# A fused linear-attention and channel-mix kernel: 1/rms from column-tiled sums of squares, spread by DMA, in a new order of work

## The chip, the core and the metric

The kernel runs on one core of one Trainium2 chip. The metric is device microseconds (us) from launch to end of one execution. Engines are called PE (TensorE), ACT (ScalarE), DVE (VectorE), POOL (GpSimd) and SP (SyncE). Each works through its own list of instructions in order. Semaphores tie the lists together.

## The reference, cut to what matters

Two stages are computed, for 8 batches (B), 8 heads (H), 576 tokens (S) and a head width of 64 (D):

```python
kv  = einsum('bhsd,bhse->bhde', k, v)
o   = einsum('bhsd,bhde->bhse', q, kv)
rms = sqrt(mean(o * o, axis=-1, keepdims=True) + 1e-06)     # per batch, head and token
x   = (o / rms * g_norm), heads side by side: (B, S, 512)
x_prev = x shifted by one token, zero at the start
xk  = mu_k * x + (1 - mu_k) * x_prev ;  xr = mu_r * x + (1 - mu_r) * x_prev
out = sigmoid(xr @ w_r) * (relu(xk @ w_k) ** 2 @ w_v)       # w_k: 512x1024, w_v: 1024x512
```

The change is about `rms`: for each token and head a sum over 64 squares, then 1/sqrt, then a product with all 64 elements of that head.

## The kernel before, in words

**Layout.** All data is held transposed: partitions are channels. The four pairs of heads (`NHP = 4`) each fill 128 partitions, 64 for either head, and are held two at a time: z = 0 holds pairs 0 and 1, z = 1 pairs 2 and 3.

**Order of work.** No scheduler runs. The kernel builds small named pieces, each a function with its dependencies, and `Plan.emit` issues them in exactly the order of the words in the string `ORDER`. A suffix @A or @D says that ACT or DVE does the piece. So each engine's list, the queue of loads on POOL and the queue of stores on SP are written out by hand in that one string. The words, for batch b, half z and token half i:

- `ld.q b.z`, `ld.k`, `ld.v`: loads from HBM, cast to bf16, issued by POOL (L247). Batches 0 and 1 load by halves z, the others whole. `ld.wk0/1`, `ld.wr`, `ld.wv0/1` load the weights (L262). `g.wk`, `g.wr` scale them by g_norm.
- `kv b`: 72 matmuls of 64x64 tiles (L282), `kc` copies the result out of PSUM. `q b.z`: 36 transposes of 64x64 (L290), `qc` copies.
- `u b.zi`: four 64x64 matmuls over 288 tokens, one section of o (L297). `uc` casts it to SBUF, `sq` squares it (L351 on ACT, L353 on DVE).
- `ss b.hp`: the sum of squares (L435). The weights are `ones`, 128x128, with 1/64 in two diagonal blocks, so every one of a head's 64 partitions gets that head's mean. Two matmuls of 288 tokens per pair of heads hp, four such words per batch from batch 1 on. Batch 0 does it by sections (L412).
- `rs b.hp`: 1/sqrt on ACT straight from PSUM (L302), 128x576 per pair of heads.
- `mul b.z`: x = o times 1/rms on DVE (L403). `wr` copies the wrap column block. `d` takes the difference to the previous token (L314), `mk`/`mr` scale it by mu (L178 on ACT, L180 on DVE), `xk`/`xr` add (L327), into a ring that holds four batches.
- `k g.fc`: x times w_k for a group g of 512 tokens (9 groups in all), four matmuls of 512 columns per word (L513; L489 for group 0). `relu` (L474), `ksq` the square (L523). `r g.ci` (L535) and `sig` (L545): the gate. `v g.ci.part` (L555): times w_v. `out` (L568, L582 in the last group): product with the gate. `st`: the stores (L464), issued by SP.
- `z:512`: a matmul of zeros, 512 columns (L453), into a PSUM tile that is not read.

**Memory that ties words together.** PSUM has two buffers "at" (u, q, kv, ss) and two buffers "mm" (k, r, v). SBUF has three buffers each for q, k, v, `sq` and `rs`, two for `sqk`. A word that needs a buffer waits for the last reader of what was in it. In the last group both column halves of `v8.3` share one PSUM tile.

**Pace.** A batch's q, k, v are loaded several batches ahead, as buffers come free. Group g can start when the batches under its 512 tokens have their `xk`. The table for 1/sqrt and the one for the sigmoid are loaded in turn on ACT (L188).

Of the kernel before, what the change touches and what calls it, by code (L numbers as in the profile page):

```python
# [20 lines left out]
g.wk11@D ss0.11 k0.010 d0.0b mr0.0a@A mul0.10 d0.1a mk0.1a@A g.wk00@D ld.wv0 rs0.11 z:512 z:512 k0.000 xk0.1a
g.wk01@D mk0.0b@A ld.wv1 mul0.11 k0.011 wr0.0@D xk0.0b d0.1b k0.001 relu0.01 ld.q2.01 mk0.1b@D q1.1 xk0.1b relu0.00
q1.0 mr0.1b@D k0.110 d0.0w xr0.0a mk0.0w@A mr0.1a@D wr0.1@A k0.111 xr0.1a ld.k2.01 g.wr1@D k0.100 mr0.0w@D relu0.11
ksq0.01 k0.101 g.wr0@D ld.v2.01 xr0.0w xr0.1b r0.0 mr0.0b@D relu0.10 xr0.0b ld.q3.01 r0.1 qc1.1@D qc1.0@A d0.1w r0.2
mr0.1w@D ld.v4.01 xk0.0w ksq0.00 r0.3 ksq0.11 sig0.0 mk0.1w@D ld.k3.01 kv1 xk0.1w ksq0.10 kc1@A u1.00 u1.11 sq1.00@A
# [5 lines left out]
ksq1.1 k1.6 relu1.2 xr1.1 ss2.3 k1.7 rs2.2 ksq1.2 rs2.3 r1.0 relu1.3 mul2.1 r1.1 wr2.1@D d2.1 q3.1 kv3 mr2.1@D q3.0
ld.k6.01 qc3.1@D r1.2 sig1.0 ld.q6.01 mk2.1@D ss2.1 qc3.0@A kc3@D r1.3 ksq1.3 v1.2.0 xk2.1 sig1.1 v1.3.0 v1.2.1
rs2.1 v1.3.1 mul2.0 u3.01 q4.1 out1.1 wr2.0@A v1.1.0 sq3.01@A uc3.01@A v1.1.1 qc4.1@D st1.2 d2.0 u3.11 u3.00
uc3.11@A v1.0.0 st0.3 mk2.0@D uc3.00@A sq3.11@D v1.0.1 sq3.00@A xk2.0 u3.10 ss3.0 sq3.10@A uc3.10@D k2.0 rs3.0
out1.0 ss3.1 k2.1 rs3.1 st1.1 ss3.3 mul3.0 k2.2 rs3.3 mr2.0@D st1.0 wr3.0@A ss3.2 relu2.0 k2.3 xr2.0 d3.0 rs3.2
st1.3 kv4 xr2.1 relu2.1 q4.0 ld.v7.01 q5.1 qc4.0@D k2.4 kc4@A ld.k7.01 qc5.1@A ksq2.1 k2.5 ld.q7.01 ksq2.0 ld.v6.01
mul3.1 u4.00 relu2.2 u4.11 k2.6 wr3.1@D uc4.00@D sq4.11@A k2.7 ksq2.2 r2.2 sq4.00@D relu2.3 uc4.11@D r2.3 d3.1
mr3.0@D u4.01 kv5 uc4.01@D q5.0 r2.0 sq4.01@D sig2.1 qc5.0@D u4.10 r2.1 kc5@A uc4.10@D ss4.1 sq4.10@D sig2.0 v2.1.0
ksq2.3 mk3.0@D ss4.3 v2.0.0 mr3.1@D mk3.1@D v2.0.1 rs4.1 xk3.0 v2.2.0 rs4.3 u5.11 u5.00 sq5.11@A uc5.11@D v2.1.1
uc5.00@A xr3.1 v2.2.1 out2.0 ss4.2 v2.3.0 rs4.2 sq5.00@D st2.0 v2.3.1 xk3.1 mul4.1 ss4.0 st2.1 k3.0 rs4.0 out2.1  # L40
q6.1 u5.10 qc6.1@D k3.1 st2.2 sq5.10@A uc5.10@A wr4.1@D k3.4 d4.1 relu3.0 st2.3 ss5.2 k3.5 rs5.2 ksq3.0 k3.2 xr3.0
relu3.2 mul4.0 k3.3 mk4.1@A mr4.1@D r3.0 ksq3.2 wr4.0@A relu3.1 r3.1 d4.0 mr4.0@D u5.01 kv6 xk4.1 q6.0 k3.6 qc6.0@D
sig3.0 k3.7 uc5.01@A kc6@A r3.2 sq5.01@D relu3.3 ksq3.1 r3.3 xr4.0 ss5.3 ksq3.3 sig3.1 ss5.1 v3.3.0 xr4.1 v3.3.1
mk4.0@D v3.2.0 rs5.3 v3.2.1 rs5.1 mul5.1 u6.11 out3.1 u6.00 uc6.11@A v3.1.0 uc6.00@A v3.1.1 sq6.11@D st3.3 wr5.1@A
xk4.0 ss5.0 v3.0.0 rs5.0 st3.2 sq6.00@A v3.0.1 u6.01 u6.10 uc6.01@A r4.0 uc6.10@A sq6.01@D r4.1 out3.0 sq6.10@A q7.1
kv7 st3.0 q7.0 r4.2 sig4.0 kc7@D mul5.0 r4.3 qc7.0@A d5.1 k4.2 mk5.1@D sig4.1 k4.3 wr5.0@A d5.0 k4.0 relu4.1 xk5.1
k4.1 qc7.1@A mk5.0@D k4.4 relu4.0 k4.5 mr5.0@A ksq4.0 k4.6 ksq4.1 k4.7 relu4.2 xk5.0 ss6.3 relu4.3 ksq4.2 ss6.2
v4.3.0 ksq4.3 v4.2.0 xr5.0 v4.2.1 rs6.3 v4.3.1 rs6.2 mul6.1 ss6.0 ss6.1 rs6.0 v4.0.0 mr5.1@D rs6.1 out4.1 v4.0.1
u7.11 u7.00 st4.2 uc7.11@D v4.1.0 uc7.00@A wr6.1@A sq7.00@D sq7.11@A v4.1.1 st4.3 u7.10 out4.0 u7.01 uc7.10@A k5.0
st3.1 uc7.01@A k5.1 sq7.10@D sq7.01@D d6.1 ss7.3 ss7.2 rs7.3 k5.2 mul6.0 relu5.0 k5.3 rs7.2 ksq5.0 ss7.1 k5.6  # L50
relu5.1 wr6.0@D mk6.1@D ss7.0 k5.7 mr6.1@A xk6.1 xr5.1 k5.4 relu5.3 mul7.1 k5.5 ksq5.1 r5.0 wr7.1@D relu5.2 d7.1
r5.1 mk7.1@D rs7.0 ksq5.3 v5.1.0 rs7.1 ksq5.2 v5.0.0 d6.0 v5.1.1 mul7.0 sig5.0 xr6.1 v5.0.1 wr7.0@A mr7.1@A r5.2
out5.0 r5.3 mk6.0@D st5.0 v5.3.0 mr6.0@D sig5.1 v5.2.0 xr6.0 st5.1 xk6.0 v5.3.1 st4.0 v5.2.1 r6.0 st4.1 out5.1 r6.1
xr7.1 st5.2 k6.4 sig6.0 d7.0 k6.5 k6.2 relu6.2 k6.3 ksq6.2 k6.0 xk7.1 relu6.1 mr7.0@D k6.1 xr7.0 r6.2 relu6.0
mk7.0@D r6.3 ksq6.1 xk7.0 k6.6 sig6.1 ksq6.0 k6.7 k8.2 relu6.3 k8.3 ksq6.3 v6.2.0 relu8.1 v6.3.0 ksq8.1 v6.3.1
v6.1.0 v6.0.0 v6.2.1 v6.1.1 out6.1 v6.0.1 k7.0 out6.0 k7.1 st6.1 r7.2 relu7.0 r7.3 st6.0 k7.2 sig7.1 st6.3 k7.3
st5.3 k8.4 relu7.1 k8.5 st6.2 ksq7.1 k7.4 ksq7.0 relu8.2 k7.5 k7.6 relu7.2 k7.7 ksq7.2 k8.0 relu7.3 k8.1 ksq7.3
v7.3.0 ksq8.2 v7.2.0 relu8.0 v7.2.1 ksq8.0 v7.3.1 v8.1.00 out7.1 k8.6 st7.3 k8.7 r7.0 st7.2 relu8.3 r7.1 ksq8.3
v7.0.0 sig7.0 v7.0.1 v7.1.0 v7.1.1 r8.0 out7.0 r8.1 st7.0 r8.2 sig8.0 r8.3 st7.1 v8.1.10 sig8.1 v8.2.00 out8.10
v8.2.10 st8.10 v8.0.00 out8.20 v8.0.10 st8.20 v8.3.00 out8.00 v8.3.10 v8.3.01 st8.00 out8.30 v8.3.11 st8.30 out8.31  # L60
st8.31
# [562 lines left out]
```

## Time and profile before

| | |
|---|---|
| time, median of 3 runs | 214.93 us (214.77 to 215.88) |
| the profiled execution's own time | 216.15 us |
| its span, first to last instruction | 214.4 us |
| around the span | 1.75 us |
| mean granted TensorE clock | 0.984 |
| PE busy | 198.5 us, 93% of the span |
| PE weight loads busy | 100.6 us, 47% |
| DVE busy | 135.0 us, 63% |
| ACT busy | 136.0 us, 63% |
| POOL busy | 26.2 us, 12% |
| moved by DMA | 26.55 MB |
| instruction fetches (queue q8) | 17, 0.28 MB |

How to read it: busy time is the union of an engine's instructions. The profile's second part cuts the span in 40 slices of 5.36 us and gives the busy tenths of each engine, the clock that PE was granted and the share of the DMA engines. The chain of work that ended last goes back from the end to what released each step; the word "issue" there is time in which the engine waited for no semaphore that the profile shows.

### The profile page before, as it was taken

To read this page: it belongs to the slowest core of one execution; us is meant where nothing else is said; L and a number is where in the kernel's file an instruction comes from. 1 tells how busy PE (TensorE), PEld (TensorE's weight loads), DVE (VectorE), ACT (ScalarE), POOL (GpSimd) and SP (SyncE) were. 2 spreads that over 40 slices of the span, in tenths; PEclk is the share of its full clock that TensorE was granted. 3 is DMA by queue.
4 is the path that set the end of the run, shared out by engine and by line. 5 is a ranking of instruction groups with operands and counts; after the bars stand their busy time and mean duration, and the time that the engine had idled before them with its cause. 6 is when DMAs were issued, how large, how long until landed. Compare 5 with 4: busy or idle time off the path is not lost.

```text
span 214.4 us, 5046 instructions
## 1 busy us (share of the span) xinstructions
PE 198.5 (93%) x2163; PEld 100.6 (47%) x2163; DVE 135.0 (63%) x260; ACT 136.0 (63%) x179; POOL 26.2 (12%) x40
## 2 busy tenths in 40 slices
PE   7966997968999999699999999999999999999991
PEld 2433773533554455244544586444444444444451
DVE  1047896595886899939975467689976432343231
ACT  2457779896886788376987889679825503533110
POOL 7833442112040040000000000000000000000000
PEclk9995799999999999999999999999999999999999
DMA  5999999999999999915302400140081004604154
GB/s 77 178 206 206 207 205 208 207 234 235 215 210 206 243 244 239 206 31 131 68 3 46 95 13 0 37 110 3 2 203 39 2 3 104 141 0 99 31 142 124
DMA packets 21370, 26.55 MB, mean 124 GB/s; under 512 B 1756, under 2 KB 16868, under 8 KB 21348
## 3 DMA queue, kind: packets, MB, share of 16 engines
q0 software_dynamic: 15408, 16.78, 46.5%
q1 hardware_dynamic: 5540, 8.92, 16.8%
q10 hardware_dynamic: 400, 0.52, 0.7%
q8 instruction: 17, 0.28, 0.5%
q14 instruction: 5, 0.04, 0.1%
...
## 4 chain that ended last, share of the span: by engine, by line
PE 86%; ACT 5%; issue 3%; DVE 2%; POOL 2%; POOLq 0%
PE mm L555 27%; PE mm L513 26%; PE mm L535 13%; PE mm L489 4%; PE at L435 3%; PE at L290 3%; PE at L297 3%; PE mm L453 2%; PE at L282 2%; PE at L555 2%; ACT sq L351 1%; DVE uT L174 1%; ACT rs L302 1%; POOL q L247 1%; ACT L188 1%
## 5 line engine op out<-in xcount | busy, mean ns | idle before, releaser
L555 PE MATMUL mm<-w_v,sqk 128*128 128x512 bf16 x272 | 62.9, 379 | 0.0
L513 PE MATMUL mm<-xk,w_k 128*128 128x512 bf16 (+1 forms) x288 | 59.5, 356 | 0.0
L474 ACT ACTIVATE relu<-mm 128x1024 bf16<-128x1024 f32 x36 | 36.9, 1027 | 25.5 <-PE mm L513 22.5
L555 PEld LDWEIGHTS <-sqk 128*128 128x128 bf16 x296 | 28.3, 98 | 31.7 <-issue 1.8
L513 PEld LDWEIGHTS <-w_k 128*128 128x128 bf16 x288 | 27.5, 98 | 24.5 <-issue 0.7
L535 PE MATMUL mm<-w_r,xr 128*128 128x512 bf16 x144 | 34.4, 379 | 1.8 <-issue 1.7
L523 DVE TENSOR_TENSOR sqk<-relu 128x1024 bf16<-128x1024 bf16 x32 | 21.5, 688 | 19.1 <-ACT relu L474 19.0
L545 ACT ACTIVATE sig<-mm 128x1024 bf16<-128x1024 f32 x18 | 18.4, 1024 | 15.8 <-PE mm L535 15.8
L568 DVE TENSOR_TENSOR out<-mm,sig 128x1024 f32<-128x1024 f32 x16 | 19.5, 1221 | 13.6 <-PE mm L555 11.7
L302 ACT ACTIVATE rs<-at,eps 128x576 bf16<-128x576 f32 (+2 forms) x32 | 22.7, 739 | 7.4 <-PE at L435 6.4
L535 PEld LDWEIGHTS <-xr 128*128 128x128 bf16 x144 | 13.6, 98 | 18.1 <-issue 2.8
L174 DVE CAST uT<-at 128x576 bf16<-128x576 f32 (+2 forms) x15 | 11.2, 759 | 16.4 <-ACT sq L351 13.4
L180 DVE TENSOR_SCALAR md<-d,cols 128x576 bf16<-128x576 bf16 (+2 forms) x58 | 17.4, 346 | 0.3
L403 DVE TENSOR_TENSOR xT<-uT,rs 128x1152 bf16<-128x1152 bf16 (+2 forms) x18 | 12.4, 687 | 7.0 <-ACT rs L302 6.8
L188 ACT ACT_TABLE_LOAD x12 | 15.4, 1283 | 0.2
L314 DVE TENSOR_TENSOR d<-xT 128x1152 bf16<-128x1152 bf16 (+2 forms) x20 | 12.7, 633 | 1.1 <-ACT xT L172 0.9
L351 ACT ACTIVATE sq<-at 128x576 bf16<-128x576 f32 (+2 forms) x17 | 10.8, 652 | 4.0 <-PE at L297 3.3
L327 DVE TENSOR_TENSOR xk<-md,xT 128x1152 bf16<-128x1152 bf16 (+2 forms) x20 | 12.6, 633 | 0.6 <-ACT md L178 0.5
L178 ACT ACTIVATE md<-d,cols 128x576 bf16<-128x576 bf16 (+2 forms) x22 | 12.8, 638 | 0.2 <-DVE d L314 0.2
L172 ACT CAST uT<-at 128x576 bf16<-128x576 f32 (+1 forms) x17 | 10.4, 637 | 3.8 <-PE at L297 3.7
L327 DVE TENSOR_TENSOR xr<-md,xT 128x1152 bf16<-128x1152 bf16 (+2 forms) x20 | 12.5, 632 | 0.2
L172 ACT COPY qT<-at 128x1152 bf16<-128x1152 bf16 (+2 forms) x9 | 9.0, 1009 | 5.3 <-PE at L290 5.3
...
## 6 DMA issues: line engine op xcount, KB each, us to landing
out_dram<-out SPq DMA_DIRECT2D x67, 128.0 KB, 2.4
...
```

The lines of the kernel that those rows point to most:

```text
L172: nc.scalar.copy(out=dst, in_=src)
L180: nc.vector.tensor_scalar(out=dst, in0=src, scalar1=col, scalar2=None, op0=ALU.mult)
L188: nc.scalar.preload_act_table_set(name)
L302: nc.scalar.activation(out=dst, in_=ps, func=AF.Abs_reciprocal_sqrt, bias=eps, scale=1.0)
L327: nc.vector.tensor_tensor(out=dst[:, 2 * z:2 * z + 2, r0:r0 + w], in0=md.t[:, :, cs], in1=xT[:, :, prev], op=ALU.add)
L474: nc.scalar.activation(out=get(rt), in_=ps.t, func=AF.Relu)
L513: nc.tensor.matmul(get(ps)[:, fc % 2, a0:a1], w_k_sb[:, cc, 128 * fc:128 * fc + 128], xk[:, cc, x0:x0 + a1 - a0], start=(cc == 0), stop=(c ...
L523: nc.vector.tensor_mul(out=get(sqk)[:, 2 * f2:2 * f2 + 2, :], in0=rt.t, in1=rt.t)
L535: nc.tensor.matmul(get(ps)[:, ci % 2, :], xr[:, cc, n0:n0 + 128], w_r_sb[:, cc, :], start=(cc == 0), stop=(cc == NHP - 1))
L545: nc.scalar.activation(out=get(sg), in_=ps.t, func=AF.Sigmoid)
L555: nc.tensor.matmul(get(ps)[:, bank, cs], sqk.t[:, fc, 128 * ci:128 * ci + 128], w_v_sb[:, fc, cs], start=(fc == 0), stop=(fc == NFC - 1))
L568: dv = add(f"out{g}.{c2}", "D", lambda _, ps=ps, sg=sg, ot=ot: nc.vector.tensor_mul(out=get(ot), in0=ps.t, in1=sg.t), deps=ms + [sg_done], ...
```

## The change

1. **Sums of squares of batches 2 to 7.** One word `ss b` per batch takes the place of four. Its weights are `heads`, 128x32, with 1/64 in column e for the 64 partitions of head e, so that each pair of heads yields two useful rows. The eight matmuls of 288 tokens (four pairs, two token halves) are each put in their own 32 columns of the array by `tile_position`, and write 32 partitions of one PSUM tile.
2. **One 1/rms.** One `rs b` on ACT, 128x576, in place of four. Its result `rsc` has one buffer. Eight of its rows carry data, one for each head.
3. **Rows spread by DMA.** `sp b.z` on SP: four DMAs, each copying one row of `rsc` (576 bf16) to 64 partitions of `rs`. Eight per batch, 48 in all. `mul` waits for them.
4. **`ORDER` is replaced** as a whole. It has 34 words `z:512` (25 before), another order of loads, another split of `uc`, `sq`, `qc`, `mk`, `mr`, `g.wk` over ACT and DVE, and other places for nearly all words. The number of k, r, v, u, q and kv words is the same. ACT loads its tables 13 times in both.
5. **Last group.** Each column half of `v8.3` gets its own PSUM tile.

PE's list has 4343 instructions (4325 before), ACT's 18 fewer `rs`.

```diff
+        "rsc": (1, (128, S), BF16),
...
+        nc.vector.memset(heads, 0.0)
+        for e in range(2):
+            nc.vector.memset(heads[64 * e:64 * e + 64, e:e + 1], 1.0 / HD)
...
+        if b >= CB:                                   # CB = 2
+            psc, rsc = Buf("at"), Buf("rsc")
+
+            def ss_heads(_):
+                for i in range(2):
+                    for hp in range(NHP):
+                        nc.tensor.matmul(get(psc)[32 * hp:32 * hp + 32, i, 0:HS], heads,
+                                         bufs[hp // 2]["sq"].t[:, hp % 2, HS * i:HS * i + HS], start=True, stop=True,
+                                         tile_position=(0, 32 * hp))
+
+            s = add(f"ss{b}", "T", ss_heads, deps=[p_setb] + [x[1] for secs in all_secs for x in secs],
+                    bufs=[psc] + [bufs[z]["sq"] for z in range(NZ)])
+            p_rsc = add(f"rs{b}", "A", lambda _: rms(_, get(rsc).rearrange("p (i c) -> p i c", i=2), psc.t[:, :, 0:HS]),
+                        deps=[s], bufs=[psc, rsc])
...
+                if b >= CB:
+                    def spread(_, z=z, rs=rs):
+                        for y in range(2):
+                            for e in range(2):
+                                r = 32 * (2 * z + y) + e
+                                nc.sync.dma_start(out=get(rs)[64 * e:64 * e + 64, y, :],
+                                                  in_=rsc.t[r:r + 1, :].unsqueeze(1).to_broadcast([1, 64, S]))
+
+                    ps_.append(add(f"sp{b}.{z}", "S", spread, deps=[p_rsc], bufs=[rsc, rs]))
-                for y in range(2):
+                for y in range(2 if b < CB else 0):
...
-                ps = Buf("at" if x else "mm")
...
                 for h, (a0, a1) in enumerate(halves):
-                    m = v_piece(f"v{g}.{ci}.0{h}", ci, 0, ps, h, slice(a0, a1), [])
+                    ps = Buf("at" if x else "mm")
+                    m = v_piece(f"v{g}.{ci}.0{h}", ci, 0, ps, 0, slice(a0, a1), [])
```

The start of the two orders, and the stretches around batch 2 and its neighbours in the new one:

```diff
-ld.q0.0 small seta setb ld.v0.0 ld.k0.0 ld.q0.1 ld.k0.1 ident ld.v0.1 id9 ld.wk1 z:512 z:512 z:512 z:512 z:512 z:512
-z:512 z:512 z:512 tr9 cols ld.wk0 z:512 q0.01 ld.q1.1 q0.00 qc0.01@A qc0.00@A table ld.q1.0 z:512 z:512 z:512 z:512
...
-q2.0 d1.0 st0.1 v0.2.0 qc2.0@A mul1.1 v0.2.1 wr1.1@D mk1.0@A d1.1 q2.1 mk1.1@D ld.q5.01 mr1.0@A xk1.0 xk1.1 qc2.1@A
-kv2 out0.1 k1.0 ld.v5.01 kc2@A st0.2 u2.01 u2.00 sq2.01@A k1.1 uc2.00@D uc2.01@A ld.k5.01 k1.2 sq2.00@D relu1.0
...
+ld.q0.0 seta small setb ld.k0.0 ld.v0.0 ld.q0.1 ld.v0.1 ld.k0.1 ident ld.wk0 id9 ld.q1.0 z:512 z:512 z:512 z:512
+z:512 z:512 z:512 z:512 z:512 z:512 z:512 q0.01 ld.wk1 tr9 qc0.01@A cols z:512 q0.00 qc0.00@A ld.v1.1 z:512 z:512
+z:512 z:512 z:512 z:512 z:512 z:512 kv0.0 ld.v1.0 kc0.0@A z:512 u0.01 u0.00 uc0.01@D uc0.00@A ld.k1.1 sq0.01@D
+sq0.00@D z:512 z:512 z:512 z:512 z:512 ss0.01 ss0.00 rs0.01 ld.k1.0 rs0.00 mul0.01 z:512 z:512 q0.11 qc0.11@D ld.wr
...
+xr0.0a u1.01 u1.00 uc1.01@A k0.111 uc1.00@A g.wr1@D ld.k3.01 g.wr0@D relu0.11 sq1.01@D r0.2 sq1.00@D ld.q3.01
...
+sq2.00@A xr1.1 relu1.3 k1.5 ksq1.3 ss2 kv3 ksq1.1 rs2 q3.0 ld.k5.01 sp2.0 r1.0 kc3@A relu1.2 qc3.0@D r1.1 ksq1.0
+u3.01 q3.1 uc3.01@D sp2.1 r1.2 ld.q6.01 sq3.01@D ld.v5.01 r1.3 sig1.0 qc3.1@D ld.v6.01 ksq1.2 u3.00 u3.10 v1.0.0
+uc3.00@D uc3.10@A st0.0 sq3.10@A sq3.00@D v1.0.1 sig1.1 mul2.0 u3.11 q4.1 wr2.0@D d2.0 v1.1.0 mk2.0@A v1.1.1 mul2.1
+v1.3.0 qc4.1@A out1.0 v1.2.0 wr2.1@A xk2.0 uc3.11@A st1.0 v1.2.1 sq3.11@A d2.1 v1.3.1 st0.3 mk2.1@D xk2.1 ss3 kv4
+out1.1 q4.0 k2.2 ld.q7.01 qc4.0@D rs3 ld.v7.01 k2.3 kc4@D sp3.0 mr2.1@D u4.11 u4.00 uc4.11@D k2.4 uc4.00@A relu2.1
...
```

More of the change, by code (lines that the diff above doesn't have):

```diff
@@ L15 @@
 ORDER = """
-ld.q0.0 small seta setb ld.v0.0 ld.k0.0 ld.q0.1 ld.k0.1 ident ld.v0.1 id9 ld.wk1 z:512 z:512 z:512 z:512 z:512 z:512
-z:512 z:512 z:512 tr9 cols ld.wk0 z:512 q0.01 ld.q1.1 q0.00 qc0.01@A qc0.00@A table ld.q1.0 z:512 z:512 z:512 z:512
-z:512 z:512 z:512 z:512 z:512 z:512 z:512 kv0.0 ld.wr kc0.0@A u0.00 u0.01 sq0.00@A uc0.00@D ld.v1.1 sq0.01@A
-uc0.01@D z:512 z:512 ss0.00 rs0.00 ss0.01 ld.k1.0 rs0.01 mul0.00 q0.10 qc0.10@D ld.k1.1 kv0.1 d0.0a q0.11 kc0.1@A
-qc0.11@D mk0.0a@A u0.10 mul0.01 u0.11 uc0.10@D sq0.10@A sq0.11@A g.wk10@D ld.v1.0 uc0.11@A ss0.10 xk0.0a rs0.10
@@ L21 @@
[L21 to L25, printed above, removed]
@@ L26 @@
-uc1.00@D sq1.11@A ld.v3.01 uc1.11@D v0.1.0 sig0.1 u1.01 u1.10 sq1.01@A uc1.01@D v0.0.0 uc1.10@A ss1.0 ld.k4.01
-v0.1.1 sq1.10@D ss1.1 v0.0.1 rs1.0 v0.3.0 rs1.1 out0.0 ld.q4.01 ss1.3 ss1.2 rs1.3 mul1.0 v0.3.1 st0.0 rs1.2 wr1.0@D
-q2.0 d1.0 st0.1 v0.2.0 qc2.0@A mul1.1 v0.2.1 wr1.1@D mk1.0@A d1.1 q2.1 mk1.1@D ld.q5.01 mr1.0@A xk1.0 xk1.1 qc2.1@A
-kv2 out0.1 k1.0 ld.v5.01 kc2@A st0.2 u2.01 u2.00 sq2.01@A k1.1 uc2.00@D uc2.01@A ld.k5.01 k1.2 sq2.00@D relu1.0
-xr1.0 u2.11 xr0.1w u2.10 uc2.11@A k1.3 uc2.10@D sq2.11@D k1.4 relu1.1 sq2.10@D mr1.1@D ss2.0 ss2.2 ksq1.0 rs2.0 k1.5
@@ L31 @@
[L31 to L60, printed above, removed]
@@ L61 @@
-st8.31
+ld.q0.0 seta small setb ld.k0.0 ld.v0.0 ld.q0.1 ld.v0.1 ld.k0.1 ident ld.wk0 id9 ld.q1.0 z:512 z:512 z:512 z:512
+z:512 z:512 z:512 z:512 z:512 z:512 z:512 q0.01 ld.wk1 tr9 qc0.01@A cols z:512 q0.00 qc0.00@A ld.v1.1 z:512 z:512
+z:512 z:512 z:512 z:512 z:512 z:512 kv0.0 ld.v1.0 kc0.0@A z:512 u0.01 u0.00 uc0.01@D uc0.00@A ld.k1.1 sq0.01@D
+sq0.00@D z:512 z:512 z:512 z:512 z:512 ss0.01 ss0.00 rs0.01 ld.k1.0 rs0.00 mul0.01 z:512 z:512 q0.11 qc0.11@D ld.wr
+mul0.00 z:512 kv0.1 q0.10 d0.0a kc0.1@A qc0.10@D mk0.0a@A z:512 u0.11 uc0.11@D u0.10 wr0.0@A sq0.10@A d0.0w sq0.11@D
@@ new lines @@
+uc0.10@A g.wk00@D ld.q1.1 z:512 z:512 z:512 z:512 ss0.10 xk0.0a d0.0b ss0.11 rs0.10 k0.000 ld.wv0 rs0.11 mul0.10
+q1.0 g.wk01@A d0.1a mk0.1a@D mk0.0b@A xk0.1a mr0.0a@D table k0.001 g.wk10@D ld.wv1 g.wk11@D k0.010 mul0.11 relu0.00
+d0.1b ld.q2.01 xk0.0b k0.011 mk0.0w@D mk0.1b@D k0.100 wr0.1@D relu0.01 xk0.1b ld.v2.01 d0.1w ksq0.00 k0.101 mr0.0b@A
+mr0.1a@D k0.110 ld.k2.01 relu0.10 xr0.0b ksq0.01 mr0.1b@A xk0.0w ksq0.10 ld.v3.01 kv1 qc1.0@D kc1@A xr0.1b mr0.0w@A
+xr0.0a u1.01 u1.00 uc1.01@A k0.111 uc1.00@A g.wr1@D ld.k3.01 g.wr0@D relu0.11 sq1.01@D r0.2 sq1.00@D ld.q3.01
@@ new lines @@
+mr0.1w@D mk0.1w@D ss1.0 xr0.0w ss1.1 ksq0.11 rs1.0 r0.3 xr0.1a rs1.1 q1.1 r0.0 qc1.1@D ld.k6.01 xr0.1w mul1.0 u1.11
+sig0.1 u1.10 r0.1 uc1.11@D sq1.10@A v0.1.0 sq1.11@D sig0.0 xk0.1w ld.q4.01 uc1.10@D ss1.2 v0.1.1 wr1.0@D d1.0 ss1.3
+v0.0.0 mk1.0@D rs1.2 xk1.0 v0.0.1 ld.v4.01 rs1.3 q2.0 mul1.1 q2.1 qc2.0@A v0.3.0 wr1.1@D d1.1 v0.3.1 out0.0 mk1.1@A
+v0.2.0 st0.1 qc2.1@A xk1.1 v0.2.1 mr1.1@D k1.2 out0.1 k1.3 mr1.0@D kv2 relu1.1 k1.0 kc2@D ld.k4.01 xr1.0 ld.q5.01
+u2.10 u2.01 uc2.10@D k1.1 uc2.01@A sq2.01@A sq2.10@D k1.6 relu1.0 u2.11 u2.00 uc2.11@A k1.7 uc2.00@D sq2.11@D k1.4
@@ new lines @@
+sq4.11@D k2.5 sq4.00@D sp3.1 mr2.0@D u4.01 relu2.2 u4.10 uc4.01@D k2.0 sq4.10@A sq4.01@D k2.1 ksq2.1 uc4.10@A st1.1
+xr2.0 ss4 relu2.0 q5.1 xr2.1 k2.6 ksq2.0 k2.7 mul3.0 qc5.1@D r2.0 relu2.3 r2.1 wr3.0@A ksq2.3 rs4 r2.2 ksq2.2 sp4.0
+d3.0 r2.3 sig2.0 mk3.0@D q6.1 mul3.1 kv5 sig2.1 q5.0 qc6.1@D st1.3 v2.3.0 kc5@A qc5.0@D v2.1.0 st0.2 wr3.1@D d3.1
+u5.11 u5.01 sp4.1 uc5.11@A v2.2.0 mk3.1@D uc5.01@A xk3.1 v2.3.1 mr3.1@D v2.2.1 sq5.01@D st1.2 sq5.11@D v2.0.0 xk3.0
+out2.1 u5.10 kv6 uc5.10@A q6.0 ld.k7.01 mul4.0 v2.0.1 st2.2 qc6.0@A mr3.0@D v2.1.1 kc6@A sq5.10@D st2.3 xr3.1 k3.2
@@ new lines @@
+out2.0 u6.10 u5.00 k3.3 uc5.00@A mul4.1 st2.0 k3.4 xr3.0 relu3.1 wr4.1@D k3.5 d4.1 uc6.10@A r3.0 mr4.1@D relu3.2
+sq5.00@D r3.1 sq6.10@D wr4.0@D ksq3.1 u6.01 sig3.0 ss5 uc6.01@D k3.0 d4.0 k3.1 sq6.01@D mk4.1@D rs5 kv7 mr4.0@D
+relu3.0 q7.0 sp5.1 xr4.0 u6.00 k3.6 kc7@A ksq3.2 qc7.0@A k3.7 mk4.0@D ksq3.0 r3.2 relu3.3 sp5.0 uc6.00@D r3.3
+sq6.00@D xk4.0 u6.11 q7.1 uc6.11@D v3.1.0 st2.1 ksq3.3 v3.0.0 sig3.1 mul5.1 v3.1.1 qc7.1@A sq6.11@D xk4.1 ss6 xr4.1
+v3.0.1 r4.0 out3.0 r4.1 rs6 st3.0 u7.10 u7.11 sq7.10@A v3.2.0 uc7.11@A st3.1 uc7.10@D v3.3.0 sq7.11@D wr5.1@D sp6.0
@@ new lines @@
+u7.00 mul5.0 u7.01 v3.2.1 sig4.0 d5.1 v3.3.1 uc7.00@A wr5.0@A k4.6 sq7.00@A out3.1 sq7.01@A k4.7 uc7.01@A mk5.1@D
+st3.2 ss7 d5.0 relu4.3 k4.2 sp6.1 mk5.0@D mr5.1@A k4.3 xk5.0 k4.4 ksq4.3 relu4.1 xr5.1 k4.5 xk5.1 k4.0 relu4.2
+mul6.0 k4.1 mr5.0@D wr6.0@A d6.0 r4.2 relu4.0 r4.3 ksq4.0 k5.2 ksq4.1 sig4.1 mul6.1 k5.3 ksq4.2 v4.1.0 mr6.0@D rs7
+xr5.0 v4.1.1 relu5.1 sp7.1 v4.0.0 wr6.1@A ksq5.1 v4.0.1 r5.0 out4.0 sp7.0 r5.1 mk6.0@D v4.3.0 d6.1 v4.2.0 mr6.1@D
+st4.1 sig5.0 mk6.1@D v4.3.1 xk6.0 v4.2.1 k5.4 out4.1 k5.5 xr6.0 st4.3 k5.0 relu5.2 xk6.1 k5.1 mul7.1 st4.0 wr7.1@A
@@ new lines @@
+k5.6 relu5.0 d7.1 st3.3 k5.7 ksq5.0 k6.6 ksq5.2 relu5.3 xr6.1 k6.7 mk7.1@D k6.0 relu6.3 mr7.1@D k6.1 ksq6.3 r6.2
+mul7.0 relu6.0 ksq5.3 r6.3 wr7.0@A xk7.1 k6.2 sig6.1 d7.0 k6.3 ksq6.0 mk7.0@A v5.1.0 relu6.1 v5.0.0 v5.0.1 v5.1.1
+r5.2 out5.0 r5.3 xk7.0 st5.0 k6.4 sig5.1 k6.5 st4.2 k7.2 relu6.2 k7.3 ksq6.2 v5.2.0 ksq6.1 relu7.1 xr7.1 v5.2.1
+v5.3.0 v5.3.1 v6.3.0 out5.1 v6.3.1 mr7.0@D st5.2 v6.2.0 ksq7.1 xr7.0 v6.2.1 st5.1 r6.0 out6.1 r6.1 st6.3 k7.4 sig6.0
+k7.5 v6.1.0 relu7.2 v6.0.0 ksq7.2 v6.0.1 v6.1.1 k8.0 out6.0 k8.1 st6.1 k8.6 relu8.0 k8.7 st5.3 ksq8.0 k7.6 relu8.3
@@ L62 @@
+st6.2 k7.7 ksq8.3 st6.0 k7.0 relu7.3 k7.1 ksq7.3 r7.0 relu7.0 r7.1 ksq7.0 k8.2 sig7.0 k8.3 v7.0.0 relu8.1 v7.0.1
+ksq8.1 v7.1.0 v7.1.1 r7.2 out7.0 r7.3 st7.1 k8.4 sig7.1 v8.1.00 st7.0 v7.3.0 v7.2.0 k8.5 v7.3.1 relu8.2 v7.2.1 r8.2
+out7.1 r8.3 ksq8.2 st7.2 r8.0 sig8.1 r8.1 st7.3 v8.2.00 sig8.0 v8.2.10 v8.1.10 out8.20 v8.0.00 st8.20 out8.10
+v8.0.10 st8.10 v8.3.01 out8.00 v8.3.11 v8.3.00 st8.00 out8.31 v8.3.10 st8.31 out8.30 st8.30
 """
@@ L132 @@
     NX = 4
+    CB = 2
     const = ctx.enter_context(tc.tile_pool(name="const", bufs=1))
@@ L195 @@
     ones = const.tile([128, 128], BF16, name="ones")
+    heads = const.tile([128, 32], BF16, name="heads")
     zero = const.tile([128, 512], BF16, name="zero")
@@ L396, in attention @@
                     qd[(z, i)] = c
+        all_secs = [[section(b, z, i, f"{b}.{z}{i}", qd[(z, i)], kvcs[z], kv, *(bufs[z][t] for t in ("qT", "uT", "sq", "rs")))
+                     for i in range(2)] for z in range(NZ)]
+        if b >= CB:
[10 more added lines that the diff above has]
+                        deps=[s], bufs=[psc, rsc])
         for z in range(NZ):
@@ L399, in attention @@
             xT, xb = xTs[(NZ * b + z) % NX], x_buf[(b, z)]
-            secs = [section(b, z, i, f"{b}.{z}{i}", qd[(z, i)], kvcs[z], kv, qT, uT, sq, rs) for i in range(2)]
+            secs = all_secs[z]
             def mul(_, cs, uT=uT, rs=rs, xT=xT):
@@ L578, in mix @@
                 for h, (a0, a1) in enumerate(halves):
-                    m = v_piece(f"v{g}.{ci}.0{h}", ci, 0, ps, h, slice(a0, a1), [])
-                    m = v_piece(f"v{g}.{ci}.1{h}", ci, 1, ps, h, slice(a0, a1), [m])
-                    dv = add(f"out{g}.{ci}{h}", "D", lambda _, ps=ps, sg=sg, ot=ot, x=x, h=h, cs=slice(a0, a1):
-                             nc.vector.tensor_mul(out=get(ot)[:, x, cs], in0=ps.t[:, h, cs], in1=sg.t[:, x, cs]),
+                    ps = Buf("at" if x else "mm")
+                    m = v_piece(f"v{g}.{ci}.0{h}", ci, 0, ps, 0, slice(a0, a1), [])
+                    m = v_piece(f"v{g}.{ci}.1{h}", ci, 1, ps, 0, slice(a0, a1), [m])
+                    dv = add(f"out{g}.{ci}{h}", "D", lambda _, ps=ps, sg=sg, ot=ot, x=x, cs=slice(a0, a1):
+                             nc.vector.tensor_mul(out=get(ot)[:, x, cs], in0=ps.t[:, 0, cs], in1=sg.t[:, x, cs]),
                              deps=[m, sg_done], bufs=[ps, sg, ot])
```

## The prediction, made before the changed kernel was run

> **What bounds it now.** I read the slices first, to see which engine is full and when.
>
> ```profile
> PE   7966997968999999699999999999999999999991
> ...
> PEclk9995799999999999999999999999999999999999
> DMA  5999999999999999915302400140081004604154
> ```
>
> PE is full from slice 10 on (50 us) but for slice 16. Before that it isn't. The DMA engines are full to slice 16 (91 us). The clock is halved in slices 3 and 4. So there are two stages: a start of some 35 us, set by loads and by the chain from one batch to the next, and then PE alone. Next the chain that ended last, for the holes in PE's stage:
>
> ```profile
> 45.48 0.41 PE at L290 x36
> 45.89 0.51 PE at L282 x56
> 46.40 2.76 issue
> 49.16 0.32 PE at L282 x16
> 49.48 0.97 PE mm L513 x4
> 50.45 0.37 PE at L297 x8
> 50.81 1.83 PE mm L513 x8
> ...
> 54.85 0.49 PE at L435 x4
> ...
> 66.81 0.25 PE at L297 x4
> ...
> 82.72 0.15 issue
> 82.87 1.46 PE mm L535 x6
> ...
> 87.24 1.66 issue
> ```
>
> Nearly every step is a matmul. The holes are "issue": PE waited for no semaphore. What they are, the page's third part and the trace's records of queue q8 tell (packets, MB, share):
>
> ```profile
> q8 instruction: 17, 0.28, 0.5%
> ```
>
> PE has 4325 instructions and 17 fetches: some 255 each. The 2.76 us hole lies before PE's 604th matmul, the 1.66 us one before its 1242nd: 638 matmuls with a weight load each are 1276 instructions, five fetches. The fetches around them start at 46.67 and 86.60 us and take 1 us. Counting back in steps of 256, a fetch is asked for when PE enters the block before, and PE goes on 5.9 us later (entered at 43.23, resumed at 49.16), 6.1 (76.79, 82.87), 6.5 (82.35, 88.89). So while DMA is full, **a block of 256 instructions must last about 6 us of PE time**, or PE stalls. The small tiles (72 matmuls in 0.6 us) use a block up fast. The three stalls cost 2.76 + 0.3 + 1.66 = 4.7 us (the middle one is a 0.53 us step in place of 0.22).
>
> **Part 1, sums of squares.** The page's rows:
>
> ```profile
> L302 ACT ACTIVATE rs<-at,eps 128x576 bf16<-128x576 f32 x28 | 19.9, 739 | 6.5 <-PE at L435 6.4
> L435 PE MATMUL at<-sq,ones 128*128 128x288 bf16 x56 | 10.5, 286 | 0.2 <-ACT rs L302 0.2
> ```
>
> Of the 28 pairs at L435, 24 go; a pair takes 0.245 us on the chain (0.49 for 4 matmuls): 5.9 us out. In come 6 x 8 matmuls of the same length, each in a quarter of the columns. If the four quarters run beside each other, eight take 0.245; if one after another, 0.98. The trace has no 32-column tile. Nearest is L297: four 64x64 tiles of 288 columns take 0.25 us alone and eight 0.37, so a further four take 0.12, the time of one. That is full overlap of four tiles, two of them side by side in columns. I take full overlap: 6 x 0.245 = 1.5 in, **net -4.4**; the other end is 0.
>
> The Trainium skill's page "TensorE: Matmul & The Clock Gate" (Part 3, "Measured speedup vs the span model") gives three column tiles 2.38 times, not 3. By that, as an estimate, a word would take 0.41 and the sum would be 1.0 us higher. The trace's row shows four tiles in the time of one, and I stay with it.
>
> A change of tile size costs too: four matmuls after a 64x64 word take 0.97 instead of 0.86, and the first u word 0.25 instead of 0.12; so 0.12 a change. From `u1.00` on the old order has 43 changes, the new one has 52 for the same words (it scatters u words, and `ss` is a third size): **+1.1**.
>
> ACT loses 18 x 0.739 = 13.3 us and seven squares. ACT is 63% busy and PE waits for it 0.5 us after 50 us, so on the path that is worth nothing. DVE takes the squares over (7 x 0.45 = 3.2 us on 135): covered likewise by its idle 37%.
>
> **Part 2, the spread.** SP issues eight DMAs per batch. SP's rows show 0.25 to 0.37 us per issue; four are about 1.1. Landing, from two windows (40 to 60 us; 90 us to the end):
>
> ```profile
> out_dram<-out SPq DMA_DIRECT2D x6, 128.0 KB, 6.5
> ...
> out_dram<-out SPq DMA_DIRECT2D x51, 128.0 KB, 2.4
> ```
>
> No row has an SBUF row copied to 64 partitions. Nearest are these stores, 64 rows each, so four take 3.5 us in the quiet part and 7.6 in the full part; the far end is the 20 us of a load in its own full queue. I take the stores. What stands behind it: `mul` waits on DVE in order, and DVE's next words are `d`, `out` and `ksq`, for which PE's `v` and both "mm" buffers wait. By PE's words the new order puts 6.1 to 13.8 us between an `sp` and its `mul` (6.4 for both of batch 2), so most is covered. Batch 2 has the least: 15.1 us of PE words from `ss2` to `k2.2`. Its chain: sum 0.25, 1/rms 0.74, eight issues 2.2, landing 6.5 is 9.7 until the second half is there; by then DVE has done `mul2.0`, and then come 5.4 us of DVE: rest of `d2.0` and `mul2.1` 1.2, `out1.0` 1.22, `xk2.0`, `d2.1`, `mk2.1`, `xk2.1` 0.75 each. That is 15.1, no margin. I add **+0.9** for it. SP's stores queue behind the spreads; `out` has three buffers, no cost. The spread moves 3.5 MB more; the load queue of the full part moves 0.2 MB/us, and the latest loads (k of batch 4, wanted about 66 us) come some 2 us early. That covers it if they share well, and costs up to 2 if not.
>
> **Part 3, fetches.** I counted the new order's PE words in steps of 256 instructions from the same offset. Up to 91 us the blocks last 7.2, 6.1, 10.5, 6.3, 7.4, 5.8, 7.9, 7.4, 6.3 and 6.8 us; the old order had 3.0, 5.3 and 4.2 where it stalled. Against 5.9 to 6.5 this leaves 0 to 1.3 us. I take 0.8: **-3.9**. If PE resumed 7 us after, with spreads in the queues, it would be 3 us again.
>
> The skill's page "Runtime: NRT & Kernel Launch" ("Instruction fetch mechanics") calls the cost of crossing a 16 KiB block mostly hidden. Here a crossing cost 2.76 us. By the page the holes would be something else, the new order would keep them, and the sum would be 3.9 higher.
>
> **Part 4, the start.** POOL's queue shows when loads land, since each later load waits for one:
>
> ```profile
> 14.15 0.71 POOL L247 DMA_DIRECT2D k<-in_k_dram  x1 [0.70 <-DMA v<-in_v_dram]
> 17.18 0.71 POOL L247 DMA_DIRECT2D v<-in_v_dram  x1 [2.32 <-DMA w_k<-in_moe_w_k_dram]
> 19.53 0.76 POOL L262 DMA_DIRECT2D w_v<-in_moe_w_v_dram  x1 [1.64 <-DMA w_k<-in_moe_w_k_dram]
> 20.92 0.74 POOL L262 DMA_DIRECT2D w_v<-in_moe_w_v_dram  x1 [0.63 <-DMA q<-in_q_dram]
> ...
> 24.94 0.74 POOL L247 DMA_DIRECT2D k<-in_k_dram  x1 [1.85 <-DMA w_r<-in_moe_w_r_dram]
> ```
>
> The first six halves are there by 14.1, then 2.7 us per half weight, 1.4 per half batch, 2.6 for w_r. In the new order w_r comes after wk0, q1.0, wk1 and four halves: 14.1 + 2.7 + 1.4 + 2.7 + 5.6 + 2.6 = 29.1. Two `g.wr` on DVE (0.51 each) and `r0.2` can start at 30.1. All of k0 fits before that: its chain ends near 29.3 by the same rows, and a halved clock there delays only words that wait for w_r anyway. So the nine added zeros and the clock are off the path: 0 either way (if the clock stays halved after 30 us, +0.9 per 1.7 us). From 30.1 the new order still has four r words (3.5), `q1.1` (0.3) and two changes (0.2) that the old one had done by 35.00, and has two u words (0.25) ahead. So it stands there at 33.85: **-1.15**. The old order then waits 0.45 and 0.35 for uT copies between its u words; the new one has k or r words there: **-0.8**, against **+0.5** for `ss1.0` behind `g.wr` on DVE.
>
> **Part 5, the end.** PE waits 0.5 us for `out` of the first column half before it may write the second half's tile. With two tiles: **-0.5**.
>
> **Sum** on the span: -4.4 + 1.1 + 0.9 - 3.9 - 1.15 - 0.8 + 0.5 - 0.5 = -8.25, so 214.4 to 206.15; with 1.75 around it 207.9 against 216.15 for the profiled execution. The median of the runs was 1.2 us under that execution: 214.93 - 8.25 = 206.7.
>
> **Rivals.**
> - *Column tiles run one after another* (no 32-column tile is in the trace; against it L297): no gain from part 1, 206.7 + 4.4 = 211.1.
> - *The fetch stalls stay or move* (blocks of 5.8 to 6.3 us against 5.9 to 6.5, more traffic in the queues): 206.7 + 3.9 = 210.6.
> - *The spread is late and DVE stands still.* For it: 64 copies from one partition are in no row, and the stores' 6.5 us are a median. Place: `mul` on DVE, then `out`, then PE's "mm" buffers. Price: landing with issue, less 6.4 us to the `mul`, less about 3.5 us that PE has in `v` words before it needs a buffer; six times. It eats the gain of 8.25 at 6.4 + 3.5 + 1.4 = 11.3 us. At 12 us: 6 x 2.1 = 12.6, so 219, slower than before; if only the three batches in the full part are hit, about 213.
> - *Better than the sum*: no margin used at batch 2, no fetch left, fewer changes paid: 204.5.
>
> **Chances.** Forecast 0.60 (205 to 208.5), tiles in series 0.10, fetches stay 0.11, spread late 0.14 (0.10 slower, 0.04 near no change), better 0.05. The range takes in all but the late spread and a little at the edges: 203.8 to 212.0. Faster or slower by over 0.5% (about what a measurement of this kernel tells from no change): faster 0.86, same 0.04, slower 0.10.
>
> **What would show it.** `ss` words of 0.25 to 0.4 us with four matmuls starting together; no "issue" hole over 0.8 us on PE before 91 us; `r0.2` at about 30 us, released by `g.wr`; landing of the spreads under 7.6 us for four, and DVE not idle at `mul` over 1 us; span near 206. A DVE wait at L403 for DMA of several us in each batch, or eight `ss` matmuls over 1 us, would make it wrong.

## The result, and the profile after

| | before | changed |
|---|---|---|
| time, median | 215.41 us (4 runs) | 270.18 us (4 runs, 269.19 to 270.64) |
| ratio | | 1.253, 95% interval 1.247 to 1.260 |
| profiled execution, span | 216.15, 214.4 us | 269.19, 267.3 us |
| PE busy, granted clock | 198.5 us, 0.984 | 204.7 us, 0.898 |

The forecast was 206.7 us. The kernel became slower by a quarter. The slices of the changed kernel, 6.7 us each, show where:

```profile
PE   8788799998209931895099348980999799999994
...
PEclk9999999999756985699669975997799999999999
DMA  6999999999999998878828878784887533160335
```

Through the first ten slices (67 us) PE is seven to nine tenths busy. Then it works in bursts up to 187 us, and with each of the five pauses its granted clock falls to 5 to 7 tenths. From 187 us on it is nearly full again. The DMA engines, which were mostly quiet from 91 us on before, are mostly seven or eight tenths busy up to 207 us. The chain of work that ended last, from 52 us on:

```profile
52.53 0.39 PE at L409 x8
52.91 0.02 issue
52.94 0.75 ACT rsc L306
53.69 0.02 issue
53.70 0.52 SPq L455
...
54.27 0.60 SPq L455
...
54.91 0.60 SPq L455
...
55.55 1.89 SPq L455
...
57.48 2.67 SPq L455
...
65.21 11.99 DMA rs<-rsc
77.21 0.03 issue
77.23 0.05 DVEq L423
...
78.00 1.23 DVE out L597
79.23 0.02 issue
79.25 5.07 DMA out_dram<-out
```

Before, nearly all of this part of the chain was PE. Now it is sums, one 1/rms, then SP issuing spreads (L455): three at 0.5 to 0.6 us each, after that one per 1.9 to 3.1 us, as if the queue had no more room. The last one lands 12 us after its issue, 23.5 us after the first was issued. Then come `mul` on DVE, `out` behind it, the store of `out`, which lands after 5.1 us, and the next batch's spreads. SP's own list says it for a whole batch, and DVE's waits say who pays:

```profile
53.70 13.84 SPq L455 DMA_DIRECT2D rs<-rsc  x8
67.59 14.07 SPq L493 DMA_DIRECT2D out_dram<-out  x6
81.75 13.92 SPq L455 DMA_DIRECT2D rs<-rsc  x8
```

```profile
DVE xT L423 <- DMA rs<-rsc: 52.2, 9, 8.9
```

Eight issues take 13.9 us, and the two stores that stand right behind them at 67.59 us need 2.9 and 3.0 us to be issued. The landing of a single spread, that is the time from its issue until its data has arrived, from the row of the tile rsc (least, median, most):

```profile
DMA to landing us min/median/max: 4.8/9.1/12.4
```

It is no effect of the loads: in the quiet part (138 to 152 us) eight again take 13.93 us, and each spread lands 10.5 us after its issue (median from 135 us on). The trace's DMA records give the pace there. About 46 packets of 1152 bytes start in each 2 us, 26.5 GB/s, and each takes 0.55 us, so some 13 of them are under way at a time. A store's packet of 2048 bytes takes 0.08 us at the median. So it is not one slow DMA engine; it looks as if many of them wait at one place. What a spread has for itself is that its 64 packets read the same SBUF row.

### The profile page after: what moved, and what is told of

Read it like the earlier page. It is cut to its first block, busy times and chain, and to the rows that moved or that the text cites. A ratio compares the mean times of both kernels' runs of the same rounds, so it can differ in the third digit from the quotient of the medians.

```text
span 267.3 us, 5107 instructions
## 1 busy us (share of the span) xinstructions
PE 204.7 (77%) x2146; PEld 99.5 (37%) x2172; DVE 138.4 (52%) x273; ACT 119.1 (45%) x151; POOL 26.5 (10%) x40
## 4 chain that ended last, share of the span: by engine, by line
PE 32%; DMA 30%; SPq 26%; ACT 4%; DVE 3%; issue 2%; POOL 1%; ACTq 0%; DVEq 0%; POOLq 0%
SPq L455 20%; DMA rs<-rsc 16%; PE mm L584 14%; PE mm L542 8%; SPq L493 6%; PE mm L564 6%; DMA w_r<-in_moe_w_r_dram 5%; DMA out_dram<-out 5%; DMA k<-in_k_dram 4%; ACT rsc L306 1%; PE at L584 1%; ACT sig L574 1%; PE at L301 1%; ACT L188 1%; DVE out L597 1%
## 5 line engine op out<-in xcount | busy, mean ns | idle before, releaser
L584 PE MATMUL mm<-w_v,sqk 128*128 128x512 bf16 x262 | 66.6, 403 | 10.4 <-DVE sqk L552 7.0
L542 PE MATMUL mm<-xk,w_k 128*128 128x512 bf16 (+1 forms) x282 | 61.1, 366 | 2.6 <-DVE out L597 1.7
L584 PEld LDWEIGHTS <-sqk 128*128 128x128 bf16 x296 | 29.3, 102 | 45.4 <-issue 10.0
L564 PE MATMUL mm<-w_r,xr 128*128 128x512 bf16 x137 | 36.0, 399 | 8.4 <-DVE xr L331 7.5
L423 DVE TENSOR_TENSOR xT<-uT,rs 128x1152 bf16<-128x1152 bf16 (+2 forms) x18 | 12.4, 689 | 54.2 <-DMA rs<-rsc 52.2
L174 DVE CAST uT<-at 128x576 bf16<-128x576 f32 (+1 forms) x14 | 10.4, 745 | 14.4 <-PE at L301 7.3
L306 ACT ACTIVATE rsc<-at,eps 128x576 bf16<-128x576 f32 x6 | 4.4, 741 | 27.5 <-DMA out_dram<-out 21.0
L409 PE MATMUL at<-sq,heads 128*32 128x288 bf16 x48 | 3.8, 337 | 15.5 <-ACT sq L355 7.9
L286 PE MATMUL at<-v,k 64*64 64x64 bf16 x576 | 7.2, 205 | 10.2 <-ACT rsc L306 8.7
L178 ACT ACTIVATE md<-d,cols 128x256 bf16<-128x256 bf16 (+2 forms) x18 | 9.9, 601 | 8.7 <-DVE d L318 8.7
L301 PE MATMUL at<-qT,kv 64*64 64x288 bf16 (+2 forms) x128 | 8.5, 315 | 5.5 <-ACT rsc L306 4.3
```

What stands on the lines that cost most here:

```text
L542: nc.tensor.matmul(get(ps)[:, fc % 2, a0:a1], w_k_sb[:, cc, 128 * fc:128 * fc + 128], xk[:, cc, x0:x0 + a1 - a0], start=(cc == 0), stop=(c ...
L564: nc.tensor.matmul(get(ps)[:, ci % 2, :], xr[:, cc, n0:n0 + 128], w_r_sb[:, cc, :], start=(cc == 0), stop=(cc == NHP - 1))
L584: nc.tensor.matmul(get(ps)[:, bank, cs], sqk.t[:, fc, 128 * ci:128 * ci + 128], w_v_sb[:, fc, cs], start=(fc == 0), stop=(fc == NFC - 1))
```

## The experiments

Theory A: a spread that reads one SBUF row 64 times is served at 26 GB/s, 2.7 us each, one after another; eight per batch hold SP's queue, DVE's `mul`, the stores and the one buffer `rsc`. Rivals: B, it is the number of DMAs or the SBUF to SBUF copy; C, the new order itself is bad. The runs that shift the fetches ask after another part of the forecast. Each ratio is to runs of the kernel before that were made along with that run (medians of 215.9 to 216.2 us).

**Spreads that read 64 different rows**

```diff
-in_=rsc.t[r:r + 1, :].unsqueeze(1).to_broadcast([1, 64, S])
+in_=rsc.t[64 * e:64 * e + 64, :]
```

> The changed kernel, with one edit: each of the 48 spreads reads 64 rows of rsc (one for each partition that it writes) in place of one row 64 times. The number of DMAs, their bytes and what waits for them stay the same; the part left out is that each head's 1/rms reaches its own partitions, so the output differs from the reference. Theory A (64 reads of one SBUF row go through one narrow place, 26 GB/s for a whole spread, and SP's queue stands behind it): a spread lands in 2 to 3 us in the quiet part, its issue takes 0.6 us, and the time falls from 270 to the prediction's sum, 205 to 209 us. Theory B (the cost lies in the number of DMAs, or in SBUF to SBUF copies of 1152 bytes, whatever their source): still about 270 us, landing about 9 us. Theory C (the new order itself is bad): the spreads get fast, the time stays over 240 us.

Measured: 210.18 us (ratio to before 0.970, 0.966 to 0.974). Landing fell as well, and SP issues eight in 5.7 us:

```profile
DMA to landing us min/median/max: 2.0/5.1/7.0
```

```profile
53.87 5.69 SPq L455 DMA_DIRECT2D rs<-rsc  x8
```

A holds, B and C fall: same number of DMAs, same bytes, same order, 60 us less. The time is 1 us over A's range; that is taken up below.

**The new order with the old sums**

```diff
-    CB = 2
+    CB = 8
-        "rs": (3, (128, 2, S), BF16),
+        "rs": (4, (128, 2, S), BF16),
-ss4 relu2.0 q5.1 xr2.1 k2.6
+ss4.0 ss4.1 rs4.0 rs4.1 relu2.0 q5.1 ss4.2 rs4.2 xr2.1 k2.6 ss4.3 rs4.3
...
```

> The changed kernel's order, with the sums of squares of all batches as before: no column tiles, no spread; the four sums and four 1/rms of a batch stand where the one sum was, the later ones one or two PE words further on, and rs has four buffers. Theory A (the spread alone costs the time): the sum of the prediction without part 1 and part 2, 206.7 + 4.4 - 0.9 = 210 us, and up to 213 us as PE waits for an at buffer until the second 1/rms is done. Theory C (the order is bad): over 225 us. If A holds, the holes named issue on PE before 91 us sum to under 1.5 us (4.6 us before).

Measured: 216.94 us (1.006, 1.003 to 1.009). C falls here too, since it is under 225. But it is 4 us over the top of the expectation (213). PE's waits, largest sum first, tell why:

```profile
PE at L465 <- ACT rs L307: 3.0, 7, 0.8
PE mm L543 <- ACT relu L504: 1.6, 1, 1.6
PE at L287 <- ACT rs L307: 1.2, 2, 0.6
...
PE at L295 <- ACT rs L307: 1.1, 2, 0.6
```

PE waited 5.3 us for 1/rms to free an "at" buffer (0.4 of it is at the start, where the 16-row run below has it too). So the fewer 1/rms on ACT, which the prediction had valued at nothing, save waits of about that size in this order, where the four stand close together. PE had no hole named issue.

**A way round by HBM**

```diff
+nc.sync.dma_start(out=bounced[b], in_=rsc.t)          # 128 rows, once per batch
-in_=rsc.t[r:r + 1, :].unsqueeze(1).to_broadcast([1, 64, S])
+in_=bounced[b][r:r + 1, :].to_broadcast([64, S])
```

> The changed kernel, with rsc written to HBM by one DMA of 128 rows per batch, and the eight spreads reading their row 64 times from HBM. Theory A (the one SBUF row is the narrow place): the write lands in about 2.4 us like a store, a spread in 2.5 to 4 us in the quiet part, the time is 206 to 211 us. Theory B (number of DMAs, or 64 copies of one row from anywhere): 265 us or more.

Measured: 219.87 us (1.015, 1.011 to 1.019). One row read 64 times from HBM is no trouble: those spreads land in 3.2 us at the median. So the repeating alone costs nothing much; repeated reads of one SBUF row do. The second hop costs instead, in the full part above all: the write is issued at 53.68 us and the first read can go at 59.56; in the quiet part that step takes 1.8 to 2.1 us. `mul` waits:

```profile
DVE xT L425 <- DMA rs<-rsd: 14.6, 5, 6.9
```

The time is 9 us over the top of A's expectation (211). I had taken 2.4 us for a write that takes 6 in the full part; that this is the whole of it was not taken apart.

**Shifting the fetches of the kernel before, to a good place and to a bad one**

```diff
-z:512 z:512 z:512 z:512 z:512 z:512 z:512 z:512 z:512 tr9
+z:64 z:64 ... (85 of them; 45 in the second run) tr9
```

> The kernel before, with one edit: the first nine matmuls of zeros with 512 columns are replaced by 85 of 64 columns, which stand in the same idle time (nine take 3.9 us, 85 at the same clock 4.5 us). That adds 152 PE instructions at the front, so each block of 256 ends at another place in the same order. Fetch theory: the blocks that lasted 3.0, 5.3 and 4.2 us of PE time become 6.2, 6.0 and 6.8; the holes named issue fall from 4.6 to under 1.5 us in all, and the time from 215 to about 211 us. Rival (the holes belong to the kv words or to something else): the holes stay at the same words and the time at 215 us.

> The kernel before, with its first nine matmuls of zeros replaced by 45 of 64 columns: 72 PE instructions more at the front, and the same idle time. The fetch theory, with 6.1 us per block, says that this is a bad place: the blocks up to 91 us then last 6.8, 8.1, 8.1, 11.1, 1.1, 15.1, 1.1 and 6.8 us of PE time, two short ones with a hole of 5 us each, 10.1 us of holes in place of 5.8 by the same sum, so the time rises by 4 us to about 219 us. Rival (more and shorter zeros are good in themselves, or the holes belong to certain words): the time is 212 to 215 us.

Measured: 211.88 us (0.978, 0.975 to 0.982) for the good place, and no hole named issue is left. 218.77 us (1.015, 1.011 to 1.019) for the bad one: the old holes are gone, and there are two at transposes that had none before, of about half the size expected:

```profile
PE at L290 <- issue: 4.8, 2, 2.5
```

No word was moved but zeros in idle time, and the holes moved or went with the steps of 256 instructions. The fetch theory holds, and its rival, that the holes belong to certain words, falls. But the 4 us of the good shift are in part luck. Word by word against the kernel before, 1.4 of its 4.3 us (of the span) are won at the very start, where the eleven zeros that were left run faster and the first `kv` starts earlier:

```profile
7.27 3.85 PE L453 MATMUL mm<-zero 128*128 128x512 bf16 x11
11.05 0.48 PE L282 MATMUL at<-v,k 64*64 64x64 bf16 x36
```

```profile
6.66 2.55 PE L455 MATMUL mm<-zero 128*128 128x512 bf16 x11
9.61 0.48 PE L284 MATMUL at<-v,k 64*64 64x64 bf16 x36 [0.40 <-DMA k<-in_k_dram]
```

The three holes of 4.7 us gave 3.0, since 0.5 us waits for `xk`, for `kc` and for a load of v came up in their place. The bad shift starts within 0.1 us of the kernel before, so its 3 us come later, where its holes are.

**16 rows per head**

```diff
-nc.vector.memset(heads[64 * e:64 * e + 64, e:e + 1], 1.0 / HD)
+nc.vector.memset(heads[64 * e:64 * e + 64, 16 * e:16 * e + 16], 1.0 / HD)
-r = 32 * (2 * z + y) + e
+r = 32 * (2 * z + y) + 16 * e
-in_=rsc.t[r:r + 1, :].unsqueeze(1).to_broadcast([1, 64, S])
+in_=rsc.t[r:r + 16, :].unsqueeze(1).to_broadcast([16, 4, S])
```

> The changed kernel, with two edits: heads has 1/64 in 16 columns for each head in place of one (the matmuls are as long as before, and 16 rows of rsc now carry the same head), and each spread reads those 16 rows four times each in place of one row 64 times. Number of DMAs, bytes and all waits stay. Theory A (one SBUF row read 64 times goes through one narrow place at 26 GB/s): with 16 rows a spread lands in 2 to 5 us in the quiet part (9 to 12 with one row, 2.0 to 7.0 with 64 rows), and the time is that of the 64-row run, 210 us; if the narrow place is shared by several neighbouring rows, a spread still occupies 1.3 us and the time is 212 to 225 us. Theory B (repeating a row at all is what costs): 260 us or more.

Measured: 208.91 us (0.970, 0.965 to 0.975). This computes all of the reference. It is the change as it was drawn, with the 30 idle columns of each tile's 32 put to use, and it is faster than both kernels. The landing, and SP's list for the same batch:

```profile
DMA to landing us min/median/max: 2.4/5.1/7.0
```

```profile
53.27 5.42 SPq L455 DMA_DIRECT2D rs<-rsc  x8
```

This run also splits the loss of the changed kernel. First the changed kernel (span 267.3 us), then 16 rows (206.5 us):

```profile
PE 204.7 (77%) x2146; PEld 99.5 (37%) x2172; DVE 138.4 (52%) x273; ACT 119.1 (45%) x151; POOL 26.5 (10%) x40
```

```profile
PE 190.0 (92%) x2146; PEld 95.3 (46%) x2172; DVE 137.7 (67%) x273; ACT 118.4 (57%) x151; POOL 26.6 (13%) x40
```

PE's idle time went from 62.6 to 16.5 us, and the same 2146 recorded matmuls took 190.0 us in place of 204.7, at a granted clock of 0.998 in place of 0.898. So of 61 us, some 46 were waiting, and some 15 went with the lower clock that the slices show at each pause.

**One row, half as many spreads**

```diff
-                        for y in range(2):
+                        for y in range(2 if z == 0 else 0):
...
+            if b >= CB:
+                rs = bufs[0]["rs"]
```

> The changed kernel (one row per head, 270.2 us), with the spreads of z = 1 left out and the 1/rms of z = 0 used for both, so the output differs from the reference. Theory A (a spread of one row takes 2.7 us of a queue that works through them one by one): four in place of eight need 11 us per batch in place of 21, near the 6.4 us that the order leaves, so most of the 60 us over the 16-row run goes: 215 to 235 us. If the time were lost to landing alone (9 us each, whatever their number), it would stay over 250 us.

Measured: 236.18 us (1.091, 1.084 to 1.099), 1 us over the range: 34 of the 61 us over the 16-row run went with half of the spreads. Against the run with half of the 16-row spreads (206.48 us, below) the 24 that are left cost 29.7 us, 1.2 us each; all 48 cost 61.3, 1.3 us each. The cost goes with their number, as in A.

**What is left over the forecast: loads**

In the 16-row run PE waited 5.0 us for loads of k, v and q; in the kernel before it never did. Two runs ask why. The first moves `kv6` and `q6.0` behind four more PE words:

> The run with 16 rows per head (208.9 us), with one stretch of the order changed: kv6, q6.0 and their copies stand 3.5 us of PE words later (behind v2.0.1, v2.1.1, k3.2 and k3.3), and u6.10 behind them. In the run before PE waited 2.4 us at kv6 for the load of v of batch 6. If what is left over the forecast of 206.7 us comes from loads that land late, this wait goes and the time falls to 206.5 to 207.5 us; if the load queue is simply full at that point and each later load is late as well, it stays at 208 to 209 us.

Measured: 210.03 us (0.974, 0.970 to 0.978), no gain, and a little over both expectations. The wait for v at `kv6` fell from 2.4 to 1.2 us, but others grew, some of them ahead of the change: from 0.3 to 1.3 us at the first `kv`, from 0.7 to 1.1 at `q3.0`. The second runs the half of the spreads, now with 16 rows:

> The run with 16 rows per head (208.9 us), with the spreads of the second half z = 1 left out: its mul takes the 1/rms of z = 0, so the output differs from the reference. 24 spreads and 1.8 MB go. If the spreads' bytes make the loads late (PE waited 5 us for loads there, 0 in the kernel before), at least half of that wait goes: 205.5 to 207 us. If the loads are late because this order asks for them earlier than the queue can bring them, the time stays at 208 to 209 us.

Measured: 206.48 us (0.956, 0.953 to 0.960). PE's waits for loads:

```profile
PE at L286 <- DMA k<-in_k_dram: 1.3, 1, 1.3
PE at L286 <- DMA v<-in_v_dram: 1.2, 2, 0.7
...
PE at L294 <- DMA q<-in_q_dram: 0.4, 1, 0.4
```

2.9 us in place of 5.0, which is less than the half expected. But 2.0 of these 2.9 come before the first spread. From `kv4` on the waits for loads fell from 3.4 us (0.9 at `kv4`, 2.4 at `kv6`) to 0.6. So about 2 us, the size of what is left over the forecast, go with half of the spreads. Whether by their bytes, which share the DMA engines with the loads, or by their number was not separated.

**A PSUM tile for each half of v8.3**, added to the good shift of the kernel before:

> The 85 short zeros in the kernel before, as in the run with 152 more instructions (211.9 us), and in the last group a PSUM tile for each column half of v8.3, as in the change. The 0.5 us wait of PE for out in the last group goes; expected 211.4 us, 0.2% under the run without it, which three rounds could hardly tell.

Measured: 211.37 us (0.980, 0.977 to 0.984), and PE's 0.5 us wait for `out` at the end is gone. The step from 211.88 is as expected, but no larger than the spread of the runs (211.07 to 211.75).

## Why the prediction was wrong, by its own steps

- **The step that failed is part 2**: "Nearest are these stores, 64 rows each, so four take 3.5 us in the quiet part and 7.6 in the full part; the far end is the 20 us of a load in its own full queue. I take the stores." The stores are like the spreads in what they write, 64 rows. They differ in what they read: 64 rows against one. Four spreads take 12.5 us in the quiet part too (issued from 138.05, `mul` at 150.52), where the prediction had 3.5, and the next four some 10 us more. The term +0.9 should have been some +60: 270.2 against 208.9 with 16 rows, on average 10 us in each of six batches. DVE's 52.2 us of waits at L423 are the sign that the prediction itself had named for being wrong.
- **The price of an issue was too low as well.** The 0.25 to 0.37 us are rows of the small loads at the start. The stores, which were taken for the landing, are issued in 0.6 us at the median in the profile before. Eight spreads took 5.4 us to issue with 16 rows, against 2.2 in the sum. There it cost little: DVE waited 1.7 us for spreads in all.
- **The rival "spread late"** named this place and its chain, `mul`, `out`, "mm" buffers, and had 0.14. Its price was far too low, since it took the late landing of one half and left out that the second half, the stores and the next `rs` stand in the same queue, and that PE's clock falls with each pause. "At 12 us" it gave 219, where 270 was measured. The range, to 212, left it out.
- **Part 1 was right.** The eight matmuls and the change of tile size take 0.35 us (52.46 to 52.81 below; 0.245 + 0.12 predicted), so all four column tiles run together, and the rival "one after another" falls. The 1.1 us for nine more changes of tile size was not tested by itself. "Worth nothing" for ACT fits the old order, where PE waited 0.7 us for 1/rms in all, but not the new one with old sums (5.3 us).

```profile
52.46 0.43 PE L409 MATMUL at<-sq,heads 128*32 128x288 bf16 x8
52.81 0.38 PE L286 MATMUL at<-v,k 64*64 64x64 bf16 x22
```

- **Part 3 was right.** In the 16-row run the longest hole named issue is 0.2 us, against 2.76 before; two shifts of the old order moved the holes with the steps of 256, though what they were worth was 3.0 us and not 4.7.
- **Part 4 was right in its main term.** `r0.2` starts at 30.40 us behind `g.wr` (30.1 predicted). The -0.8 and +0.5 behind it were not checked one by one:

```profile
30.40 0.81 PE L564 MATMUL mm<-w_r,xr 128*128 128x512 bf16 x2 [0.67 <-DVE w_r L180]
```

- **Part 5 was right**: the 0.5 us wait went with the second tile; in the time it is not clear of the spread.
- **Covered loads**: "costs up to 2 if not". They were not covered, and it cost about 2.

With the spread mended 208.9 us was measured, where the whole sum gives 206.7. That the run with half of the spreads comes to 206.5 is no proof of the sum, since it leaves out a part of the work. The change as drawn was sound but for one access pattern.

Two things stay open. How many rows share the narrow place was not tried: 16 neighbouring rows are enough to be rid of it, and 2 to 8 rows were not run. But the trace of the changed kernel speaks against one place for each row. From 138 us on the spreads read rows 64, 65, 96, 97 and then 0, 1, 32, 33, and the same again from 186 us on. If each row had its own place, two rows could be read side by side at every passage from one to the next. Yet the packets stay at 0.55 us at all passages but one: from row 97 to row 0 (149 to 150 us, and again at 197) some 45 packets take under 0.1 us. So the four rows of a half seem to share one place, and the two halves to have one each, though the buffer that is written changes at that passage too. If it is so, spreads that alternate between the halves would also go faster; no run tried it. And how much of the 61 us is DVE's wait and how much the stores behind the spreads was not taken apart.
